# Two pairs of token blocks that take turns by halves of the inner tiles, in a spectral mixer with an MLP on one Trainium2 core

## The chip, the core and the metric

The kernel runs on 1 core of a Trainium2 chip. TensorE (PE in the profile; PEld is its weight load) multiplies, VectorE (DVE), ScalarE (ACT) and GpSimd (POOL) work elementwise, SyncE (SP) issues nearly all DMAs from one queue that it works off in order. The metric is the time of one execution on the device in microseconds (us).

## The reference

```python
X = np.fft.rfft(x, axis=1)                    # x: 8 x 3072 x 256
Yr = Xr @ w_r - Xi @ w_i + b_r                # complex 256 x 256 mix
Yi = Xr @ w_i + Xi @ w_r + b_i
Y  = sign(Y) * maximum(abs(Y) - 0.01, 0)      # real and imaginary part each
y  = np.fft.irfft(Y, n=3072, axis=1)          # tokens: 24576 x 256
h  = y @ w_in                                 # 256 -> 2048
g  = maximum(h, 0) + log1p(exp(-abs(h)))      # softplus
out = g @ w_out                               # 2048 -> 256
```

## The kernel before

All data is fp32. From the second batch on, and in the MLP throughout, a factor is split into a high part (fp32r, `hi`) and the rest (`lo`), and `mm3` (L207) issues three matmuls: hi by hi, hi by lo, lo by hi.

**The transform** of a batch goes in five steps of products, each with its evacuations: `s1` (16 products over the 96 points), `s3` (12, the 32 points), `mix` (12, the 256 x 256 mix with bias and shrinking), `s4` (12), `s5` (4 for each pair of token blocks). Between s1 and s3 the data goes through DRAM (`a_dr`), between s4 and s5 as well (`d_dr`, read back as `dp` tiles by `load_d`).

**The MLP** works on a *key* (batch, pair, mp): a pair of two token blocks of 512 tokens (3 pairs in a batch) and one of 8 inner tile pairs of 256 of the 2048 inner columns. The first layer of a key is 7 products in place of 8 (sums of weight blocks S1 to S4 and of token blocks T1 to T4): for one pair `s5` gives four PSUM tiles, and `b11`, `b12`, `b22`, `b21` (L496 to L518) make from them the seven split token tiles in `y_sb`. ACT and DVE snap, add and softplus the results (L530 to L554, tiles `psc` and `pse`), split them (`gh`, `gl`), and the second layer (`ffn2`, L556) adds them up in PSUM (`pso`, 2 banks for a block, 4 in all) over the 8 mp of a pair. After the last one `ffn2` copies the sums out into two `ot` tiles for a block and stores them.

**The weights** of the first layer (`w_in`, `which` = 1) and of the second (`which` = 0) come in 8 pieces each. A conversion, `split_w` (L146), turns one piece into float, sums and hi and lo parts in several steps on ACT, DVE and POOL, writes them in the tile `wp` (one buffer; `w_1` in the tile y1 for w_in while the start lasts), and stores them in DRAM (`w_dr`, L195). Its helper tile `wu` (L155) has the buffers of `ot` (tag "ot", two). `stream_w` (L200) reads a piece back for each key.

**The order** is written out by hand in *slots*. A key has four slots; slot 0 is the first of the MLP, and the slots before it are the start. In a slot the engines get, in this order: the first-layer products (`slot_products`), the due steps of conversions (`before`: a `yield` puts the rest into the next slot), at most one product of the transform (`steps`), loads and splits (`fill`), what an earlier slot put off (`later`), and the second-layer products (`slot_second`). Every engine works off its own list in order. The plan for the start is the list `first` (L671 to L681): s1 of batch 0 and four of batch 1, s3, mix and s4 of batch 0, six more s1 of batch 1, and s5 of pair 0. Nine conversions begin in the start, five slots apart, and seven more at slots 1, 4, ..., 19. Pair 1 of batch 0 is made ready (`plan_s5`) around slots 18 to 24, the remaining s1 of batch 1 run from slot 1, its s3, mix and s4 from slot 14.

Of the kernel before, what the change touches and what calls it, by code (L numbers as in the profile page):

```python
# [17 lines left out]
P = 128  # L18
# [3 lines left out]
BLK = 512  # L22
# [11 lines left out]
def tile_spectral_mixer_mlp(ctx, tc, x, w_r, w_i, bias, bias_0, w_in, w_out, f, f_hi, f_lo, g1, g3, g3_hi, g3_lo, hm, out):  # L34
# [61 lines left out]

    def store(dst, src, what):

        def start():
            nc.sync.dma_start(dst, src)  # L100
            stored[what] += 1

        later.append(start)
# [121 lines left out]
    def load_x(b, c):  # L225

        if b == 0 or (b, c // 10) == (1, 0):
# [15 lines left out]
    def s1(b, c):  # L243
# [17 lines left out]
        if b == 0:  # L261
            stored["a", b] += 1
        else:
            store(a_dr[b][:, 2 * c:2 * c + 2, :].rearrange("(g q) n c -> q g n c", q=4), a.rearrange("p (n c) -> p n c", n=2), ("a", b))

# [182 lines left out]
    def s5(b, blk, k):  # L448
# [3 lines left out]
        while t < (blk + 1) * BLK:  # L452
# [8 lines left out]
            t += n  # L461
        (b11, b21, b12, b22)[blk % 2 * 2 + k]((b, blk // 2), ps)

# [29 lines left out]
    def put_split(*args):  # L493
        split_token(*args) if early else later.append(lambda: split_token(*args))

# [7 lines left out]
    def b12(key, ps):  # L503
        difference(0, ps)
        keep(key, 1, ps)
        put_split(key, T1, 0, nc.vector if early else nc.gpsimd)

    def b22(key, ps):
        whole(key, B22, ps)
        difference(1, ps)  # L510
        difference(0, ps)
        put_split(key, T2, 0, nc.vector if early else nc.gpsimd)
        put_split(key, T3, 1, nc.vector)

    def b21(key, ps):
        whole(key, B21, ps)
        difference(0, ps)
        put_split(key, T4, 0, nc.vector if early else nc.gpsimd)  # L518

# [30 lines left out]
    def low(key, what):  # L550
# [64 lines left out]
    def slot_second(s, key, prev):  # L615
        if s < 3:
            if prev:
                what = (C22, C12, C21)[s]
                ffn2(prev, what, what == C22 and prev[2] == 0, what != C22 and prev[2] == NM // 2 - 1)
                if s == 2:  # L620
                    del w_t[0, prev]
        elif key:
            ffn2(key, C11, key[2] == 0, False)
            del w_t[1, key]


    with tc.manual_schedule():
# [17 lines left out]
        def plan_s1(b, start, step, first=0):  # L645
            for c in range(first, 16):
                t = product(start + step * (c - first), s1, b, c)
                at(t - 3, split_x, b, c)
                at(t - 7, load_x, b, c)

        def plan_mix(b, start, step):
            mixed = done = start
            for gp in range(NP):
                t = product(max(start + step * gp, mixed), s3, b, gp)
                at(max(t - 4, 11), load_a, b, gp)
                mixed = product(max(t + (3 if gp else 4), done + 1), mix, b, gp)
# [198 lines left out]
```

## Time and profile before

| | us |
|---|---|
| median of 3 runs | 2681.21 (2679.93 to 2683.26) |
| the profiled execution: its own time | 2679.82 |
| its span, first to last instruction | 2678.0 |
| PE busy | 2603.8 |

The trace of the profiled execution is read here by stages, cut at times at which a slot begins on PE: slot 0 at 131.07 us, slot 4 at 157.72, slot 16 at 205.46, slot 26 at 261.40 and slot 42 at 321.10. A view by stages gives each engine's busy time and the clock granted to TensorE (1.00 is 2.4 GHz). A view of waits names the instruction that waited and what released it. In a timeline the bracket behind a row is the idle time before it.

### The profile page before, as it was taken

What the parts mean: (1) busy time and instruction counts of PE and PEld (TensorE: products, weight loads), DVE (VectorE), ACT (ScalarE), POOL (GpSimd) and SP (SyncE); (2) the same over time, 40 slices, a digit from 0 to 9 for tenths busy, and PEclk for the clock granted to TensorE, in tenths of its full rate; (3) what the DMA queues carried; (4) which work ended last, traced back from release to release, by engine and by line L of the source; (5) the groups of instructions that cost most, each with busy time, mean ns of one, the idle gap of its engine ahead of it and who ended that gap; (6) DMA issues with size and microseconds to landing.
All of it is one profiled execution on the core that took longest, in us unless ns stands there. A gap on an engine that the chain in (4) does not pass through costs nothing.

```text
span 2678.0 us, 36264 instructions
## 1 busy us (share of the span) xinstructions
PE 2603.8 (97%) x13059; PEld 2184.2 (82%) x13059; DVE 1626.2 (61%) x2701; ACT 1719.5 (64%) x3115; POOL 301.3 (11%) x292
## 2 busy tenths in 40 slices
PE   7768999999999999999999999999999999999999
PEld 5546888888888888888888888888888888888887
DVE  3666665666646666566665666556665666645454
ACT  3365666666666666666676666666666666666665
POOL 2432110110101101101011011010010000000000
PEclk8889999999999999999999999999999999999999
DMA  6766556556455565564555644646455455445543
GB/s 191 254 210 206 194 164 198 166 187 193 157 188 178 178 198 170 179 205 156 184 172 172 217 159 153 220 163 198 164 167 191 155 170 188 142 154 183 186 147 110
DMA packets 186116, 479.73 MB, mean 179 GB/s; under 512 B 18097, under 2 KB 86961, under 8 KB 185937
## 3 DMA queue, kind: packets, MB, share of 16 engines
q1 hardware_dynamic: 185376, 476.95, 55.1%
q8 instruction: 103, 1.69, 0.3%
q0 software_dynamic: 560, 0.47, 0.1%
q14 instruction: 77, 0.62, 0.1%
HBM read 390.31 MB, written 83.89 MB: 177 GB/s over the span
## 4 chain that ended last, share of the span: by engine, by line
PE 88%; DVE 2%; DMA 2%; ACT 1%; issue 0%; POOL 0%; SPq 0%; DVEq 0%; ACTq 0%; POOLq 0%
PE pso L208 13%; PE pso L209 12%; PE pso L210 12%; PE psc L208 6%; PE psc L210 6%; PE psc L209 6%; PE pse L208 5%; PE pse L210 5%; PE pse L209 5%; PE psf L455 4%; PE psf L209 4%; PE psf L208 4%; PE psf L210 4%; PE psf L287 2%; DMA w_dr<-wp 1%; DVE shrunk L413 0%
## 5 line engine op out<-in xcount | busy, mean ns | idle before, releaser
L553 DVE TENSOR_TENSOR gl<-t,gh 128x512 fp32r<-128x512 f32 x768 | 533.2, 694 | 349.7 <-ACT gh L547 346.8
L532 ACT COPY t<-psc 128x512 f32<-128x512 f32 x576 | 337.0, 585 | 504.4 <-PE psc L210 502.4
L537 DVE TENSOR_TENSOR t<-pse,t 128x512 f32<-128x512 f32 x576 | 396.2, 688 | 426.9 <-ACT t L532 278.3
L208 PE MATMUL pso<-gh,w 128*128 128x512 f32 x1536 | 616.2, 401 | 0.0
L209 PE MATMUL pso<-gl,w 128*128 128x512 f32 x1536 | 600.0, 391 | 0.0
L210 PE MATMUL pso<-gh,w 128*128 128x512 f32 x1536 | 599.5, 390 | 0.0
L547 ACT CAST gh<-t 128x512 fp32r<-128x512 f32 x768 | 476.8, 621 | 58.2 <-PE pso L210 34.4
L543 ACT ACTIVATE t<-t 128x512 f32<-128x512 f32 x576 | 364.5, 633 | 58.7 <-DVE t L537 58.0
L210 PEld LDWEIGHTS pso<-gh,w 128*128 128x128 f32 x1536 | 288.7, 188 | 62.5
L208 PEld LDWEIGHTS pso<-gh,w 128*128 128x128 f32 x1536 | 290.1, 189 | 54.9
L209 PEld LDWEIGHTS pso<-gl,w 128*128 128x128 f32 x1536 | 290.0, 189 | 51.4
L208 PE MATMUL psc<-y_sb,w 128*128 128x512 f32 x768 | 301.6, 393 | 16.1 <-DMA w<-w_dr 7.8
L210 PE MATMUL psc<-y_sb,w 128*128 128x512 f32 x768 | 300.1, 391 | 0.0
L209 PE MATMUL psc<-y_sb,w 128*128 128x512 f32 x768 | 299.6, 390 | 0.0
L208 PE MATMUL pse<-y_sb,w 128*128 128x512 f32 x576 | 227.8, 396 | 14.4 <-DVE t L537 7.9
L115 POOL TENSOR_TENSOR xl<-xt,xh 96x512 fp32r<-96x512 f32 x102 | 134.1, 1317 | 938.3 <-ACT xh L106 783.6
L209 PE MATMUL pse<-y_sb,w 128*128 128x512 f32 x576 | 225.2, 391 | 0.0
L210 PE MATMUL pse<-y_sb,w 128*128 128x512 f32 x576 | 225.1, 391 | 0.0
L489 POOL TENSOR_TENSOR y_sb<-raw,y_sb 128x512 fp32r<-128x512 f32 x69 | 92.3, 1337 | 1128.5 <-ACT y_sb L486 1124.9
L208 PEld LDWEIGHTS psc<-y_sb,w 128*128 128x128 f32 x768 | 144.5, 188 | 51.0 <-ACT t L532 10.2
L210 PEld LDWEIGHTS psc<-y_sb,w 128*128 128x128 f32 x768 | 144.6, 188 | 31.0
L209 PEld LDWEIGHTS psc<-y_sb,w 128*128 128x128 f32 x768 | 144.6, 188 | 29.7
(131 smaller groups left out, 3637.8 us busy)
## 6 DMA issues: line engine op xcount, KB each, us to landing
w<-w_dr SPq DMA_DIRECT2D x192, 896.0 KB
w<-w_dr SPq DMA_DIRECT2D x192, 512.0 KB
dp<-d_dr SPq DMA_DIRECT2D x80, 384.0 KB
xt<-in_x SPq DMA_DIRECT2D x128, 192.0 KB
d_dr<-d SPq DMA_DIRECT2D x96, 256.0 KB
out_y<-ot SPq DMA_DIRECT2D x96, 256.0 KB
ap<-a_dr SPq DMA_DIRECT2D x84, 256.0 KB
a_dr<-a SPq DMA_DIRECT2D x102, 192.0 KB
```

The lines of the kernel that those rows point to most:

```text
L115: (eng or nc.vector).tensor_tensor(out=lo, in0=src, in1=hi.bitcast(F32), op=ALU.subtract)
L208: nc.tensor.matmul(ps, wh, xh, start=start, stop=False, skip_group_check=more)
L209: nc.tensor.matmul(ps, wh, xl, start=False, stop=False, skip_group_check=more)
L210: nc.tensor.matmul(ps, wl, xh, start=False, stop=stop, skip_group_check=more)
L287: nc.tensor.matmul(xv[:, g, k], t[:, g, k * P:(k + 1) * P], g1_t[:, g].rearrange("p (c s) -> p c s", c=2), start=True, stop=True,)
L455: nc.tensor.matmul(ps[:, t - blk * BLK:t - blk * BLK + n], d_sb[b, blk // 2, n2 // 4][0][:, n2 % 4, k * P:(k + 1) * P], d_sb[b, blk // 2, ...
L489: eng.tensor_tensor(out=lo, in0=raw[j], in1=hi.bitcast(F32), op=ALU.subtract)
L532: nc.scalar.copy(t, banks[bank])
L537: nc.vector.tensor_tensor(out=t, in0=banks[bank], in1=t, op=ALU.add)
L543: nc.scalar.activation(t, banks[bank] if bank else t, AF.Softplus)
L547: nc.scalar.copy(gh, ct[key, what])
L553: nc.vector.tensor_tensor(out=gl, in0=ct.pop((key, what)), in1=gh.bitcast(F32), op=ALU.subtract)
```

## The change

- **Turns.** In batch 0, pairs 0 and 1 take turns: pair 0 with mp 0 to 3, pair 1 with mp 0 to 3, pair 0 with mp 4 to 7, pair 1 with mp 4 to 7. Pieces 4 to 7 of the weights are first needed at slot 32 in place of slot 16.
- **Accumulators in DRAM.** After its first four mp a pair's sums are copied into `ot` tiles and stored (`part_dr`); `load_part` reads them back one slot ahead of the last products of the second half, and DVE adds them to PSUM in place of the copies.
- **Pair 1 earlier.** Its s5 products run in slots 2, 5, 7 and 10, its eight `dp` loads from slot -2.
- **Tokens of pair 0.** s5 runs in the order b11, b21, b12, b22, and `first_tokens` makes the tiles in another order of ACT and DVE instructions. B21 is kept in a third `raw` tile.
- **Conversions.** Six begin in the start, seven slots apart; ten more at slots 0, 3, 6, 10, 14, ..., 34. The store stands one step later.
- **The start** has four s1 of batch 1 behind s4 in place of six; these and the other s1 of batch 1 come from slot 0, loaded 5 slots ahead in place of 7.

```diff
 def load_w(which, m2):
-        if m2 < 6:
+        if m2 < 3:
 def split_w(which, m2):
         v.tensor_tensor(out=lo, in0=src, in1=hi.bitcast(F32), op=ALU.subtract)
+        yield
         nc.sync.dma_start((w1_dr if which else w2_dr)[m2][:, :], w.bitcast(F32))
 def s5(b, blk, k):
-        (b11, b21, b12, b22)[blk % 2 * 2 + k]((b, blk // 2), ps)
+        if early:
+            first_tokens((b, blk // 2), blk % 2 * 2 + k, ps)
+        else:
+            (b11, b21, b12, b22)[blk % 2 * 2 + k]((b, blk // 2), ps)
+    def first_tokens(key, i, ps):
+        v = nc.vector
+        if i == 0:
+            b11(key, ps)
+        elif i == 1:
+            whole(key, B21, ps)
+            raw[2] = sb.tile([P, BLK], F32, tag="d", name="raw")
+            nc.scalar.copy(raw[2], ps)
+        elif i == 2:
+            b12(key, ps)
+        else:
+            difference(0, ps)
+            difference(1, ps)
+            for j, t in ((0, T2), (1, T3)):
+                nc.scalar.copy(tokens(key, t)[0], raw[j])
+            nc.scalar.copy(tokens(key, B22)[0], ps)
+            for j, t in ((0, T2), (1, T3)):
+                hi, lo = tokens(key, t)
+                v.tensor_tensor(out=lo, in0=raw[j], in1=hi.bitcast(F32), op=ALU.subtract)
+            hi, lo = tokens(key, B22)
+            v.tensor_tensor(out=lo, in0=ps, in1=hi.bitcast(F32), op=ALU.subtract)
+            v.tensor_tensor(out=raw[2], in0=raw[2], in1=raw[0], op=ALU.subtract)
+            put_split(key, T4, 2, v)
+    def turns(key):
+        return key[:2] in ((0, 0), (0, 1))
+    def begins(key):
+        return key[2] == 0 or turns(key) and key[2] == NM // 4
+    def ends(key):
+        return key[2] == NM // 2 - 1 or turns(key) and key[2] == NM // 4 - 1
+    def load_part(blk):
+        partial[blk] = []
+        for k in range(2):
+            t = sb.tile([P, BLK], F32, name="part", **(dict(tag="d") if blk % 2 else dict(tag=f"r{k}", bufs=1)))
+            nc.sync.dma_start(t, part_dr[blk, k][:, :])
+            partial[blk].append(t)
 def ffn2(key, what, first, last):
                 ot = sb.tile([P, BLK], F32, tag="ot", name="ot")
-                if k == 0:
+                if blk in partial and not b:
+                    nc.vector.tensor_tensor(out=ot, in0=o[k], in1=partial[blk][k], op=ALU.add)
+                elif k == 0:
                     nc.scalar.copy(ot, o[k])
                 else:
                     nc.vector.tensor_copy(ot, o[k])
-                store(out[b, blk, k], ot, "out")
+                if mp == NM // 2 - 1:
+                    store(out[b, blk, k], ot, "out")
+                else:
+                    part_dr[blk, k] = dram.tile([P, BLK], F32, tag=f"part{blk}{k}", name="part_dr", bufs=1)
+                    store(part_dr[blk, k][:, :], ot, ("part", blk, k))
...
         for j in range(NM):
-            t = t0 + 23 + 5 * j if j < 9 else 1 + 3 * (j - 9)
+            t = t0 + 22 + 7 * j if j < 6 else 3 * (j - 6) if j < 8 else 6 + 4 * (j - 8)
...
         keys = [(b, bp, mp) for b in range(B) for bp in range(NPAIR) for mp in range(NM // 2)]
+        keys.sort(key=lambda key: (not turns(key), turns(key) and key[2] // (NM // 4), key))
+        for bp in range(2):
+            t = 4 * keys.index((0, bp, NM // 2 - 1))
+            at(t + 4, load_part, 2 * bp + 1)
+            at(t + 5, load_part, 2 * bp)
```

**ACT around the tokens of pair 0**, the last slots of the start; `y_80` is the s1 output of batch 1, `wu`, `w_962` and `wp` belong to a conversion. Before:

```order
L260 COPY y_80<-psf 96x512 x4
L474 CAST y_sb<-psf 128x512
L479 COPY raw<-psf 128x512
L158 ACTIVATE wu<-w_962 128x512
L161 ACTIVATE w_962<-w_962 128x512
L192 CAST wp<-wp 128x512
L479 COPY raw<-psf 128x512
L486 CAST y_sb<-raw 128x512
L474 CAST y_sb<-psf 128x512
L486 CAST y_sb<-raw 128x512 x2
L106 CAST xh<-xt 96x512
L474 CAST y_sb<-psf 128x512
```

The first L474 here is B11, the last one B21, which the second product of slot 0 needs. After:

```order
L261 COPY y_80<-psf 96x512 x3
L479 CAST y_sb<-psf 128x512
L484 COPY raw<-psf 128x512
L479 CAST y_sb<-psf 128x512
L509 COPY raw<-psf 128x512
L106 CAST xh<-xt 96x512
L192 CAST wp<-wp 128x512
L484 COPY raw<-psf 128x512
L491 CAST y_sb<-raw 128x512
L106 CAST xh<-xt 96x512
L516 CAST y_sb<-raw 128x512 x2
L517 CAST y_sb<-psf 128x512
```

B21 (the second L479) now comes second, and three copies of s1 stand ahead (of the stretch shown) in place of four.

**SP around slot 0**, up to the read of the first-layer weights for key 1 (`w1_dr1`). `xt` are the inputs of s1, `w64` raw weights, `w2_dr2` and `w2_dr3` stores of conversions. Before:

```order
L143 DMA w64_1043<-in_w_out 128x2x512
L231 DMA xt_1046<-in_x 96x512
L195 DMA w2_dr3_92<-wp_995 128x1024
L231 DMA xt_1071<-in_x 96x512
L143 DMA w64_1103<-in_w_in 128x2x512
L231 DMA xt_1106<-in_x 96x512
L204 DMA w1_1108<-w1_dr1_82 128x1792
```

After:

```order
L232 DMA xt_1006<-in_x 96x512
L442 DMA dp_1008<-in_hm 96x384
L443 DMA dp_1008<-d_dr_367 96x1024
L442 DMA dp_1011<-in_hm 96x384
L443 DMA dp_1011<-d_dr_367 96x1024
L442 DMA dp_1014<-in_hm 96x384
L443 DMA dp_1014<-d_dr_367 96x1024
L442 DMA dp_1017<-in_hm 96x384
L443 DMA dp_1017<-d_dr_367 96x1024
L232 DMA xt_1038<-in_x 96x512
L196 DMA w2_dr2_91<-wp_952 128x1024
L205 DMA w1_1069<-w1_dr1_82 128x1792
```

Eight loads for pair 1 (2.1 MB) and one store of a conversion have come ahead of the weights for key 1; two raw weight loads are gone from there.

**ACT where sums are copied out.** Before, this happens first in slots 33 and 34:

```order
L532 COPY t<-psc 128x512
L572 COPY ot<-pso 128x512
L532 COPY t<-psc 128x512
L330 COPY sum<-psf 128x256
L301 CAST lh<-psf 128x2x256
L106 CAST sh<-shrunk 128x512
L572 COPY ot<-pso 128x512
```

After, it happens first in slots 17 and 18:

```order
L303 CAST lh<-sum 128x2x128
L625 COPY ot<-pso 128x512
L562 COPY t<-psc 128x512
L158 ACTIVATE wu<-w_1637 128x512
L161 ACTIVATE w_1637<-w_1637 128x512
L625 COPY ot<-pso 128x512
L573 ACTIVATE t<-t 128x512
```

Between the two copies a conversion now takes one of the two `ot` buffers for `wu`, and holds it for two slots; the same happens in slots 33 and 34.

## Rows read from the trace of the kernel before

**Rows 1.** The page, engine totals: busy us, share of the span, instructions.

```profile
PE 2603.8 (97%) x13059; PEld 2184.2 (82%) x13059; DVE 1626.2 (61%) x2701; ACT 1719.5 (64%) x3115; POOL 301.3 (11%) x292
```

**Rows 2.** The view by stages, one row for each: from and to, length, busy time (and count) of PE, PEld, DVE, ACT and POOL, granted clock, DMA share, GB/s.

```profile
0.00:106.92 106.92, 85.95 (x451) 64.58 (x452) 60.12 (x96) 42.48 (x78) 38.13 (x42) 0.90 0.66 213
106.92:131.07 24.15, 17.52 (x61) 12.59 (x60) 6.32 (x13) 7.81 (x14) 7.40 (x9) 0.65 0.86 263
131.07:157.72 26.65, 11.71 (x34) 7.29 (x35) 17.77 (x29) 14.56 (x27) 11.07 (x10) 0.69 0.49 162
157.72:205.46 47.74, 38.76 (x156) 29.02 (x156) 31.79 (x58) 32.32 (x57) 14.49 (x10) 0.95 0.66 237
205.46:261.40 55.94, 44.54 (x222) 37.13 (x221) 36.39 (x64) 28.06 (x51) 12.00 (x15) 0.91 0.65 208
261.40:321.10 59.70, 59.04 (x310) 50.03 (x308) 42.70 (x76) 38.86 (x74) 5.15 (x4) 1.00 0.58 191
321.10:2678.00 2356.90, 2346.27 (x11833) 1983.52 (x11831) 1431.08 (x2369) 1555.37 (x2815) 213.09 (x204) 1.00 0.54 175
```

**Rows 3.** PE's timeline, single rows: start, length, instruction, idle time before it and its releaser.

```profile
119.88 1.99 PE L455 MATMUL psf<-dp 96*128 96x96 f32 x8 [5.95 <-DMA dp<-d_dr]
131.07 0.77 PE L208 MATMUL psc<-y_sb,w 128*128 128x512 f32 x1
...
139.20 0.79 PE L208 MATMUL pse<-y_sb,w 128*128 128x512 f32 x1 [6.50 <-ACT y_sb L474]
...
157.72 0.77 PE L208 MATMUL psc<-y_sb,w 128*128 128x512 f32 x1 [7.14 <-DMA w<-w_dr]
...
205.46 0.39 PE L208 MATMUL psc<-y_sb,w 128*128 128x512 f32 x1
205.69 0.39 PE L209 MATMUL psc<-y_sb,w 128*128 128x512 f32 x1
...
228.56 0.58 PE L208 MATMUL psf<-wmh,lh 128*128 128x256 f32 x1 [5.93 <-ACT raw L479]
```

**Rows 4.** ACT's timeline around the tokens of pair 0.

```profile
125.88 0.58 ACT L260 COPY y<-psf 96x512 f32<-96x512 f32 x1 [12.38 <-DMA a_dr<-y]
...
128.23 0.58 ACT L474 CAST y_sb<-psf 128x512 fp32r<-128x512 f32 x1
...
138.57 0.57 ACT L474 CAST y_sb<-psf 128x512 fp32r<-128x512 f32 x1
```

**Rows 5.** The timelines of POOL and of SP's queue ahead of slot 4, and last a line of SP's waits in the first 300 us (sum, times, longest).

```profile
149.39 1.31 POOL L165 TENSOR_TENSOR wu<-w,wu 128x512 f32<-128x512 f32 x1 [6.40 <-ACT xh L106]
150.65 3.39 POOL L115 TENSOR_TENSOR xl<-xt,xh 96x512 fp32r<-96x512 f32 x2
...
152.40 0.31 SPq L231 DMA_DIRECT2D xt<-in_x  x1
152.77 0.42 SPq L204 DMA_DIRECT2D w<-w_dr  x1
...
SPq L231 <- POOL xl L115: 17.8, 3, 8.5
```

**Rows 6.** The stage from 72 us to the last s4, by the view by stages.

```profile
72.00:106.92 34.92, 27.80 (x169) 22.02 (x168) 31.91 (x50) 13.42 (x25) 18.92 (x16) 0.95 0.77 255
```

**Rows 7.** A line of PE's waits in the first 262 us (sum, times, longest).

```profile
PE psf L427 <- POOL z L382: 4.9, 3, 2.2
```

**Rows 8.** DVE's groups from 131 to 262 us: count | busy, mean ns of one | idle before them and its releaser.

```profile
L194 DVE TENSOR_TENSOR wp<-wp 128x512 fp32r<-128x512 f32 (+1 forms) x8 | 6.7, 833 | 0.0
L163 DVE SCALAR_TENSOR_TENSOR wt<-wu,wt 128x512 f32<-128x512 f32 x8 | 5.5, 684 | 0.0
...
L160 DVE SCALAR_TENSOR_TENSOR wt<-w,wt 128x512 uint32<-128x512 uint32 x7 | 4.8, 693 | 0.2
L182 DVE TENSOR_TENSOR wp<-wt,wu 128x512 f32<-128x512 f32 x4 | 4.6, 1160 | 6.0 <-DMA w_dr<-wp 6.0
...
L164 DVE TENSOR_SCALAR wu<-wt 128x512 uint32<-128x512 uint32 x8 | 3.4, 427 | 0.3
...
L159 DVE TENSOR_SCALAR wt<-w 128x512 uint32<-128x512 uint32 x7 | 2.9, 420 | 0.0
...
L178 DVE TENSOR_TENSOR wp<-wt,wu 128x256 f32<-128x256 f32 x3 | 1.3, 426 | 10.1 <-DMA w_dr<-wp 10.1
```

**Rows 9.** Pieces of the chain that ended last, from 100 to 270 us: start, length, what.

```profile
216.49 8.79 DMA w_dr<-wp
240.79 4.63 DMA w_dr<-wp
253.91 1.31 PE psf L455 x12
262.24 0.89 PE psf L287 x8
```

**Rows 10.** The view of the tile `ot`, 280 to 310 us: durations min/median/max in ns, first and last start; last, who waited for its stores.

```profile
L572 ACT COPY ot<-pso x2: 587/594/601, 290.3 to 293.8; 128x512 f32<-128x512 f32 x2
L574 DVE COPY ot<-pso x2: 691/691/691, 292.5 to 295.4; 128x512 f32<-128x512 f32 x2
...
DVE ot L574: 0.6, 1
```

More of the change, by code (lines that the diff above doesn't have):

```diff
@@ L95, in put_off, with store @@
         later.append(f) if early else f()
-    def store(dst, src, what):
+    def store(dst, src, what, eng=None):
         def start():
-            nc.sync.dma_start(dst, src)
+            (eng or nc.sync).dma_start(dst, src)
             stored[what] += 1
@@ L225, in load_x @@
     def load_x(b, c):
-        if b == 0 or (b, c // 10) == (1, 0):
+        if b == 0 or (b, c // 8) == (1, 0):
             xt = sb.tile([P, 512], F32R, tag=("gh", "gl")[c % 2], name="xt", bufs=3).bitcast(F32)[:N1]
@@ L263, in s1 @@
         else:
-            store(a_dr[b][:, 2 * c:2 * c + 2, :].rearrange("(g q) n c -> q g n c", q=4), a.rearrange("p (n c) -> p n c", n=2), ("a", b))
+            store(a_dr[b][:, 2 * c:2 * c + 2, :].rearrange("(g q) n c -> q g n c", q=4), a.rearrange("p (n c) -> p n c", n=2), ("a", b),
+                  None)
     def load_a(b, gp):
@@ L493, in put_split @@
     def put_split(*args):
-        split_token(*args) if early else later.append(lambda: split_token(*args))
+        later.append(lambda: split_token(*args))
+    def first_tokens(key, i, ps):
[21 more added lines that the diff above has]
+            put_split(key, T4, 2, v)
     def b11(key, ps):
@@ L505, in b12 @@
         keep(key, 1, ps)
-        put_split(key, T1, 0, nc.vector if early else nc.gpsimd)
+        (split_token if early else put_split)(key, T1, 0, nc.vector if early else nc.gpsimd)
     def b22(key, ps):
@@ L511, in b22 @@
         difference(0, ps)
-        put_split(key, T2, 0, nc.vector if early else nc.gpsimd)
+        put_split(key, T2, 0, nc.gpsimd)
         put_split(key, T3, 1, nc.vector)
@@ L517, in b21 @@
         difference(0, ps)
-        put_split(key, T4, 0, nc.vector if early else nc.gpsimd)
+        put_split(key, T4, 0, nc.gpsimd)
     gt, po, ct, banks = {}, {}, {}, {}
@@ L554, in low @@
         gt[key, what] = gh, gl
+    def turns(key):
[4 more added lines that the diff above has]
+        return key[2] == NM // 2 - 1 or turns(key) and key[2] == NM // 4 - 1
+    part_dr, partial = {}, {}
+    def load_part(blk):
+        partial[blk] = []
+        for k in range(2):
+            assert stored["part", blk, k] == 1
+            t = sb.tile([P, BLK], F32, name="part", **(dict(tag="d") if blk % 2 else dict(tag=f"r{k}", bufs=1)))
+            nc.sync.dma_start(t, part_dr[blk, k][:, :])
+            partial[blk].append(t)
     def ffn2(key, what, first, last):
@@ L618, in slot_second @@
                 what = (C22, C12, C21)[s]
-                ffn2(prev, what, what == C22 and prev[2] == 0, what != C22 and prev[2] == NM // 2 - 1)
+                ffn2(prev, what, what == C22 and begins(prev), what != C22 and ends(prev))
                 if s == 2:
@@ L622, in slot_second @@
         elif key:
-            ffn2(key, C11, key[2] == 0, False)
+            ffn2(key, C11, begins(key), False)
             del w_t[1, key]
@@ L648, in plan_s1 @@
                 at(t - 3, split_x, b, c)
-                at(t - 7, load_x, b, c)
+                at(t - (5 if b == 1 else 7), load_x, b, c)
         def plan_mix(b, start, step):
@@ L654, in plan_mix @@
                 t = product(max(start + step * gp, mixed), s3, b, gp)
-                at(max(t - 4, 11), load_a, b, gp)
+                at(max(t - 4, 14), load_a, b, gp)
                 mixed = product(max(t + (3 if gp else 4), done + 1), mix, b, gp)
@@ L659, in plan_s5 @@
         def plan_s5(b, bp, start):
-            if (b, bp) == (1, 0):
+            if (b, bp) in ((0, 2), (1, 0)):
                 start += 3
@@ L667, in plan_s5 @@
                 t = product(t + 2, s5, b, 2 * bp + j, k)
-            assert t + 2 < NT * b + 2 * NM * bp, (b, bp, t)
+            assert t + 2 < NT * b + (NM if (b, bp) == (0, 1) else 2 * NM * bp), (b, bp, t)
         first = [("s1", 0, c) for c in range(16)] + [("s1", 1, c) for c in range(4)]
@@ L678, in tile_spectral_mixer_mlp @@
                 first.append(("mix", 0, i - 1))
-        first += [("s1", 1, c) for c in range(4, 10)]
-        first += [("s5", j, k) for j, k in ((0, 0), (1, 0), (1, 1), (0, 1))]
+        first += [("s1", 1, c) for c in range(4, 8)]
+        first += [("s5", j, k) for j, k in ((0, 0), (0, 1), (1, 0), (1, 1))]
         t0 = -len(first)
@@ L703, in tile_spectral_mixer_mlp @@
         for j in range(NM):
-            t = t0 + 23 + 5 * j if j < 9 else 1 + 3 * (j - 9)
-            at(t - (6 if j < 9 else 4 if j < 12 else 2), load_w, (j + 1) % 2, j // 2)
+            t = t0 + 22 + 7 * j if j < 6 else 3 * (j - 6) if j < 8 else 6 + 4 * (j - 8)
+            at(t - (6 if j < 6 else 8 if j < 7 else 2), load_w, (j + 1) % 2, j // 2)
             before.setdefault(t, []).append(split_w((j + 1) % 2, j // 2))
@@ L717, in tile_spectral_mixer_mlp @@
         nt = NT
-        plan_s1(1, 1, 1.6, 10)
+        plan_s1(1, 0, 1.6, 8)
         for b in range(B):
             for bp in range(1, NPAIR):
-                plan_s5(b, bp, nt * b + 2 * NM * bp - 14)
+                plan_s5(b, bp, nt * b + (NM if (b, bp) == (0, 1) else 2 * NM * bp) - 14)
             if b + 1 < B:
-                plan_mix(b + 1, *((14, 4.9) if b == 0 else (nt * b - 4, 5.6)))
+                plan_mix(b + 1, *((16, 4.9) if b == 0 else (nt * b - 4, 5.6)))
                 plan_s5(b + 1, 0, nt * (b + 1) - 14)
```

## The prediction

> **What bounds the kernel now.** I read the engine totals first. PE is busy 97% of the span [rows 1], so nothing that leaves its products alone can move the time except where PE waits or runs at the low clock. The view by stages says where that is [rows 2]: from 321.10 us on PE idles 10.6 us in 2357, and from slot 26 to 42 0.7 in 59.7, at a clock of 1.00. In the 261 us before, it idles 62.9 and the clock drops as far as 0.65. So the place of the change is the place of the loss, and only these stages need to be worked out.
>
> How much is lost there? One second-layer matmul follows another in 0.23 us at the full clock (the two rows at 205 us) [rows 3]. A key has 45 of them, 10.3 us, 2.6 a slot; key 0 has only 27 in its slots 0 to 3. An s1 is three, 0.7 us; an s5 takes 1.3 and an s3 0.9 [rows 9]. With these:
> - slots 0 to 3: 27 x 0.23 + 2 s1 = 7.6 us of work in 26.65: 19.0 lost;
> - slots 4 to 15: 12 x 2.6 + 4 s1 + an s3 = 34.9 in 47.74: 12.8 lost;
> - slots 16 to 25: slots 26 to 41, with the same transform work beside them, take 59.70 / 16 = 3.73 each; ten and four s5 are 42.5, in 55.94: 13.4 lost.
>
> The waits name the causes. Slot 0 has a product that waits 6.50 us for B21 [rows 3]: ACT copies it only at 138.57, after all other tiles; and ACT itself had stood 12.38 us behind stores of s1 output when s5 was already running, so that B11 came at 128.23, s5 having begun at 119.88 [rows 3, 4]. Slot 4 waits 7.14 us for its weights, which SP issued at 152.77, held up by an x load whose buffer waited for POOL, which had stood behind a conversion's multiply [rows 5]. In slots 4 to 25 DVE waits 6.0 + 10.1 = 16.1 us for the store of the conversion before, since `wp` has one buffer [rows 8]; the longest, a store of 8.79 us [rows 9], ends in PE's wait of 5.93 at 228.56 [rows 3]. Before all that, from 72 us to the last s4, DVE is busy 31.91 of 34.92 us, mostly with conversions, and PE 27.80 [rows 6].
>
> **The change part by part**, against the profiled execution (2679.82 us, 1.4 below the median).
>
> *1. Start: -6 us (0 to -11).* Six conversions for nine, every seventh slot for every fifth, take some 30% of DVE's conversion work out of a stage in which DVE is 91% busy and PE loses 7.1 us [rows 6], 4.9 of it over the start waiting for z, which comes through DVE [rows 7]. I take 4. Then s5 waits 5.95 us for `dp` [rows 3] with the DMA engines at a share of 0.86 [rows 2]; two raw weight loads (0.5 MB each), a weight store and two x loads leave: I take 2. If the wait is the latency of the last store and load, nothing comes; the upper end is 7.1 and two thirds of 5.95. The two s1 that leave had that wait behind them, so nothing is won by their going, and in slots they cost 2 x 0.7: *+1.4*.
>
> *2. Slots 0 to 3: -14.6 us (-6 to -19).* With four s1 in the start no copy waits for a store of the first four, so ACT is free when s5 ends its tiles; B21 is second, and the 6.50 goes. What is late next is the chain through T2: two differences, T2's copy and rest, T3's, B22's and T4's DVE work and the add of the first result, eight pieces of 0.6 to 0.7 (copies 0.58 in rows 4, DVE 0.68 in rows 8), 5.2; softplus, split and snap 1.8; product S1 and its snap 2; the add, the last two products at the low clock and the add for the next key 4, with a conversion's sums between, 1 more: 14 us. Work in it is 9.6 (one more s1, one s5), so 4.4 is lost for 19.0. The weights for key 1 stand behind eight `dp` loads now; 2.1 MB at the 263 GB/s of rows 2 are 8 us and the weights 3.5 more, about 12 after their first issue just ahead of slot 0: just in time. Low end: only the 6.50 goes. High end: all goes.
>
> *3. Slots 4 to 15: -1 us (-9 to +8).* Tokens of pair 1 (some eleven DVE and ten ACT pieces of 0.6 to 0.7) come in from slots 18 to 24; conversions are at three slots' distance until slot 6. There the next one writes `wp` one slot (3.7 us) after the last rest, and the store takes 4.6 to 8.8 [rows 9], as before: I expect one wait like the 8.37 hidden in the 10.1 of rows 8 around slot 5. From slot 10 on four slots' distance gives two slots (7.5 us) against 4.6: those waits go. Lost: 12 for 12.8.
>
> *4. Slots 16 to 41: +1 us (-10 to +35).* The 13.4 goes with the `wp` waits and with pair 1's tokens. Two things come. First, conversions now run to slot 39 beside s3, mix and s4. DVE is busy 42.70 / 16 = 2.67 us a slot there [rows 2]; a conversion has 3.7 us of DVE in the rows (29.2 us for some eight [rows 8]; the small sums of a w_in piece come on top), 0.9 a slot: 3.6 or more of 3.73. It fits, but an in-order engine that full makes PE wait: 8 us, an estimate from slots 4 to 15, where DVE at 31.79 of 47.74 went with 12.8 lost. Second, in slots 17, 18 and 33, 34 `wu` holds one of the two `ot` buffers, so the second block's two copies pass one after the other through the other buffer: copy, store, copy, store, copy. A store costs at most 2.2 us with little else queued, from the end of DVE's first copy (292.5 + 0.7) to the next, which waited for it at 295.4 [rows 10], 4.6 in company [rows 9]; copies are 0.6 and 0.7. The last copy is out 3.5 to 6.0 us after the last product; PE needs the bank after two first-layer products and one of the transform, some 2.8. So 0.7 to 3.2 a time; SP has a weight store and weights ahead, I take 3.2: 6.4. Sum 14.4 for 13.4.
>
> *5. The way back: +3 us (0 to +8).* The adds stand in for copies of the same length. But `load_part` is issued one slot ahead: for pair 0 its second half is behind weights (0.9 MB) and three `dp` pairs (1.6 MB), 10 us at 263 GB/s, with the add due in three slots, 11. DVE stands in order behind it with `gl` and the adds that PE needs: 2; for pair 1, with less ahead, 1. The trace of before has no such load; the nearest is the 4.6 of rows 9, with which it would be hidden. The Trainium skill, "DMA: Bandwidth & Descriptors", Rules for kernel authors, says the opposite of this placing: issue the DMA early, compute, wait late. Its fit of 2.0 us + bytes / 436 GB/s (section Anatomy of one DMA, taken on another queue) gives 4.1 us for a 0.9 MB store that took 4.63 here, and 9.6 for the second half: by it this term would be 0 to +1, and the sum 2 to 3 lower.
>
> The eight extra copies (0.6 each), 4 MB of DMA out and back and the longer second half of the weights lie in stages with DMA at 0.54 to 0.65 [rows 2] and ACT at two thirds: hidden; if not, 8 x 0.6.
>
> Sum: -6 + 1.4 - 14.6 - 1 + 1 + 3 = -16.2, so 2663.6 for a profiled execution, **2665** as a median.
>
> **Rivals.**
> *More: all `wp` waits go and DVE's load hides.* For it: slots 26 to 41 lose nothing with DVE at 72%. Terms 3 and 4 would be -10 and -10: 2665 - 20 = 2645.
> *The first wait is replaced.* If the x loads and conversion store that now stand before key 1's weights are late, as the x load was that waited up to 8.5 us [rows 5], or the `dp` loads fill the DMA engines longer, slot 4 begins 25 us after slot 0 and not 14. That gives 2676, within 0.2%. Against it: the first two x splits now stand ahead of the conversion's multiply on POOL.
> *DVE becomes the bound in slots 16 to 41, slower than before.* If the pace of slots 16 to 25, 5.6 us a slot, came not from `wp` but from conversions, mix and second-layer splits crossing on DVE, the change stretches it over 26 slots: 26 x (5.6 - 3.73) = 49 lost for the 14 of term 4, 2700. It decides from a pace of 3.73 + (14.4 + 16) / 26 = 4.9. For it: the sum of 3.6 or more of 3.73, and L182, 1160 ns where other 512-wide pieces take 690 [rows 8]. Against it: DVE was idle a third of slots 16 to 25. The Trainium skill, "GPSIMD Engine Reference", section 1 Specifications, has VectorE and GpSimd share SBUF interfaces, with contention where a DVE instruction has two SBUF inputs. The mean of L182 agrees; by that rule every DVE piece beside a POOL multiply stretches and this rival gains.
>
> **How the numbers follow.** Chances: forecast 0.64, more 0.12, replaced wait 0.14, DVE bound 0.10. The forecast's own range is 2652 to 2675. The range goes to 2645, where the second case lies, and over the third to 2684, half way to the last. What a measurement can tell from no change is about 0.2%, 5.4 us: faster 0.76, same 0.14, slower 0.10.
>
> **What would show it.** Step 1: slot 0 begins near 125 us. Step 2: no product waits for B21, slot 4 begins 13 to 16 us after slot 0. Step 3: DVE waits for `w_dr` once for long, near slot 5, and hardly from slot 12 on. Step 4: slots 16 to 41 at some 4.2 us; second-layer products in slots 19 and 35 wait 2 to 4 us for copies. Step 5: an add waits for `part_dr`. I am wrong if slot 4 still begins 25 us after slot 0, if slots 16 to 41 take 4.9 or more, or if a wait appears past slot 68.

## The result

The changed kernel takes **2708.8 us** (median of 4 runs, 2704.2 to 2709.5) against 2680.6 for the kernel before on the same chip (4 runs, 2679.5 to 2683.3): ratio 1.010, 95% interval 1.0083 to 1.0118. It is slower by 28 us; the prediction said 16 us faster, and its range ended at 2684.

The page's engine totals of the changed kernel, in the columns of [rows 1]:

```profile
span 2706.2 us, 36340 instructions
PE 2616.3 (97%) x13061; PEld 2192.6 (81%) x13061; DVE 1635.0 (60%) x2716; ACT 1725.3 (64%) x3118; POOL 298.0 (11%) x287
```

PE idles 2706.2 - 2616.3 = 89.9 us where it idled 74.2 [rows 1], 15.7 more. It is also busy 12.5 us longer with the same products (13061 records, 13059 before): their granted clock was lower, 0.979 over the span where it had been 0.987. Together they are the 28.2 us by which the span grew.

Where? The view by stages of the changed kernel, in the columns of [rows 2], cut where slots 0, 4, 16, 42 and 72 begin on PE:

```profile
104.50:124.39 19.89, 17.29 (x58) 12.36 (x57) 5.61 (x9) 8.21 (x14) 3.75 (x5) 0.59 0.80 240
124.39:145.30 20.91, 17.16 (x51) 12.20 (x50) 12.57 (x25) 12.75 (x25) 7.17 (x6) 0.61 0.96 284
145.30:206.94 61.64, 43.15 (x188) 33.51 (x187) 37.10 (x57) 36.29 (x66) 20.37 (x13) 0.86 0.51 169
206.94:331.04 124.10, 102.20 (x476) 82.71 (x475) 90.00 (x164) 72.99 (x133) 21.86 (x21) 0.89 0.61 210
331.04:460.00 128.96, 115.45 (x578) 96.71 (x576) 80.64 (x136) 73.52 (x134) 11.78 (x9) 0.93 0.54 173
460.00:2706.00 2246.00, 2237.65 (x11272) 1892.95 (x11270) 1355.94 (x2243) 1482.69 (x2677) 199.93 (x194) 1.00 0.54 175
```

In the kernel before the same slots begin at 131.07, 157.72, 205.46, 321.10 [rows 2] and, slot 72, at 433.48, by this row of PE's timeline:

```profile
433.48 0.39 PE L208 MATMUL psc<-y_sb,w 128*128 128x512 f32 x1
```

Stage against stage:

| stage | before | after | difference | the prediction's term |
|---|---|---|---|---|
| start, to slot 0 | 131.1 | 124.4 | -6.7 | -6 |
| slots 0 to 3 | 26.7 | 20.9 | -5.7 | -14.6 |
| slots 4 to 15 | 47.7 | 61.6 | +13.9 | -1 |
| slots 16 to 41 | 115.6 | 124.1 | +8.5 | +1 |
| slots 42 to 71 | 112.4 | 129.0 | +16.6 | +3 |
| from slot 72 | 2244.5 | 2246.2 | +1.7 | 0 |

(The prediction's +1.4 for two s1 moved into slots is in no one stage.) The gain at the beginning is there, though smaller; the loss lies at five places. PE's timeline of the changed kernel, as in [rows 3]:

```profile
171.30 0.79 PE L209 MATMUL psc<-y_sb,w 128*128 128x512 f32 x1 [13.00 <-ACT t L562]
...
225.81 0.74 PE L209 MATMUL psc<-y_sb,w 128*128 128x512 f32 x1 [2.71 <-ACT t L573]
226.34 0.63 PE L210 MATMUL psc<-y_sb,w 128*128 128x512 f32 x1
226.77 0.63 PE L211 MATMUL psc<-y_sb,w 128*128 128x512 f32 x1
231.75 0.80 PE L209 MATMUL pse<-y_sb,w 128*128 128x512 f32 x1 [4.36 <-DVE t L567]
...
238.75 0.39 PE L209 MATMUL psc<-y_sb,w 128*128 128x512 f32 x1
...
306.06 0.80 PE L209 MATMUL pse<-y_sb,w 128*128 128x512 f32 x1 [7.39 <-DVE t L567]
...
372.65 0.80 PE L209 MATMUL pse<-y_sb,w 128*128 128x512 f32 x1 [5.75 <-DVE t L567]
...
443.00 0.80 PE L209 MATMUL pse<-y_sb,w 128*128 128x512 f32 x1 [5.07 <-DVE t L567]
```

The wait of 13.00 ends where slot 7 begins. The others lie in slots 20, 36, 52 and 68, each time at the first `pse` product, two slots after the last products of a turn. These four slots take 12.9, 15.0, 11.0 and 12.7 us (slot 20: 225.81 to 238.75); in the fastest run below they take 6.1, 7.4, 3.4 and 4.9. The brackets name ACT and DVE, but both were waiting themselves. DVE's timeline says for what:

```profile
152.23 1.08 DVE L194 TENSOR_TENSOR wp<-wp 128x896 fp32r<-128x896 f32 x1
153.24 1.80 DVE L583 TENSOR_TENSOR gl<-t,gh 128x512 fp32r<-128x512 f32 x1
168.34 0.69 DVE L182 TENSOR_TENSOR wp<-wt,wu 128x512 f32<-128x512 f32 x1 [13.29 <-DMA w_dr<-wp]
...
229.81 0.69 DVE L627 COPY ot<-pso 128x512 f32<-128x512 f32 x1 [7.38 <-DMA part_dr<-ot]
...
304.11 0.69 DVE L627 COPY ot<-pso 128x512 f32<-128x512 f32 x1 [9.06 <-DMA part_dr<-ot]
...
370.08 1.31 DVE L623 TENSOR_TENSOR ot<-pso,part 128x512 f32<-128x512 f32 x2 [6.08 <-DMA out_y<-ot]
...
439.44 0.69 DVE L623 TENSOR_TENSOR ot<-pso,part 128x512 f32<-128x512 f32 x1 [5.93 <-DMA out_y<-ot]
```

One wait is for the store of a conversion, whose `wp` the next one wants; four are for stores of results, whose `ot` buffers are wanted again. In slots 52 and 68 the second block's results wait for the stores of the first block's. In slots 20 and 36 the last result waits for the store of the one just before it, of the same block: `wu` of a conversion held the other buffer. ACT made that copy, and had itself waited for a store before, to give `wu` its buffer (2.76 us, until 222.40; PE's 2.71 ahead of slot 20 stands behind that):

```profile
223.50 0.58 ACT L625 COPY ot<-pso 128x512 f32<-128x512 f32 x1
```

Behind these four waits stands, in DVE's order, the add of a first-layer result (L567) that frees the bank PE needs; behind the wait for `wp` stands a difference of tokens (L487, 168.95), which ACT's copy of `psc` (L562) came after. And SP's queue, where these stores were issued:

```profile
154.52 0.37 SPq L143 DMA_DIRECT2D w<-in_w_in  x1
156.19 0.32 SPq L232 DMA_DIRECT2D xt<-in_x  x1
156.60 0.38 SPq L205 DMA_DIRECT2D w<-w_dr  x1
157.03 0.61 SPq L100 DMA_DIRECT2D a_dr<-a  x1
157.74 0.41 SPq L196 DMA_DIRECT2D w_dr<-wp  x1
...
224.29 6.56 SPq L100 DMA_DIRECT2D part_dr<-ot  x2
...
361.44 1.24 SPq L604 DMA_DIRECT2D part<-part_dr  x2
363.02 1.86 SPq L100 DMA_DIRECT2D out_y<-ot  x2
```

Conversion 6's store could have gone at 153.3, when its rest was done; it stood 4.4 us behind a raw weight load, which waited for POOL, and an x load, and then took 10.6 (157.74 to 168.34) with 1.8 MB issued just ahead of it. It is the change that put it there: the `yield` ahead of the store moves it from slot 4 to slot 5, behind the loads of slot 4. No run takes that line back by itself. The stores of `ot` took 229.81 - 224.29 = 5.5 us and 370.08 - 363.02 = 7.1; before, at most 2.2 [rows 10].

### The profile page after: what moved, and what is told of

Read it like the earlier page. It is cut to its first block, busy times and chain, and to the rows that moved or that the text cites. A ratio compares the mean times of both kernels' runs of the same rounds, so it can differ in the third digit from the quotient of the medians.

```text
span 2706.2 us, 36340 instructions
## 1 busy us (share of the span) xinstructions
PE 2616.3 (97%) x13061; PEld 2192.6 (81%) x13061; DVE 1635.0 (60%) x2716; ACT 1725.3 (64%) x3118; POOL 298.0 (11%) x287
## 4 chain that ended last, share of the span: by engine, by line
PE 81%; DVE 1%; ACT 1%; DMA 1%; issue 0%; SPq 0%; DVEq 0%
PE pso L209 12%; PE pso L211 12%; PE pso L210 12%; PE psc L209 6%; PE psc L211 6%; PE psc L210 6%; PE pse L209 4%; PE pse L211 4%; PE pse L210 4%; PE psf L457 4%; PE psf L210 3%; PE psf L209 3%; PE psf L211 3%; PE psf L289 2%; DVE shrunk L415 0%; DMA out_y<-ot 0%
## 5 line engine op out<-in xcount | busy, mean ns | idle before, releaser
L583 DVE TENSOR_TENSOR gl<-t,gh 128x512 fp32r<-128x512 f32 x768 | 536.3, 698 | 333.6 <-ACT gh L577 330.7
L567 DVE TENSOR_TENSOR t<-pse,t 128x512 f32<-128x512 f32 x576 | 396.1, 688 | 437.0 <-ACT t L562 284.1
L562 ACT COPY t<-psc 128x512 f32<-128x512 f32 x576 | 337.8, 586 | 480.6 <-PE psc L211 478.7
L210 PEld LDWEIGHTS psc<-y_sb,w 128*128 128x128 f32 x768 | 145.4, 189 | 29.8
```

The source lines that it names most:

```text
L210: nc.tensor.matmul(ps, wh, xl, start=False, stop=False, skip_group_check=more)
L562: nc.scalar.copy(t, banks[bank])
L567: nc.vector.tensor_tensor(out=t, in0=banks[bank], in1=t, op=ALU.add)
L583: nc.vector.tensor_tensor(out=gl, in0=ct.pop((key, what)), in1=gh.bitcast(F32), op=ALU.subtract)
```

## The experiments

Each time is a median beside runs of the kernel before on the same chip (2680.5 to 2680.9), with the ratio to it. Stage lengths are read as above, from the starts of slots in each trace. In the runs that leave the changed start as it is (all but start_only and warm) slot 0 begins between 119.5 and 124.7 us; differences of a few us there are taken as scatter, so causes are read from single stages.

| run | us | ratio (95%) | slots 0-3 | 4-15 | 16-41 | 42-71 |
|---|---|---|---|---|---|---|
| before | 2680.6 | 1 | 26.7 | 47.7 | 115.6 | 112.4 |
| after | 2708.8 | 1.010 (1.0083 to 1.0118) | 20.9 | 61.6 | 124.1 | 129.0 |
| own_ot | 2685.5 | 1.0021 (1.0012 to 1.0029) | 20.4 | 62.7 | 109.3 | 124.2 |
| later7 | 2699.4 | 1.0071 (1.0059 to 1.0084) | 20.2 | 47.2 | 131.7 | 128.5 |
| both | 2674.6 | 0.9976 (0.9967 to 0.9986) | 20.5 | 45.3 | 113.0 | 124.7 |
| start_only | 2679.7 | 0.9997 (0.9988 to 1.0006) | 21.1 | 50.8 | 119.2 | 110.0 |
| part_early | 2700.7 | 1.0077 (1.0063 to 1.0091) | 20.0 | 61.9 | 123.5 | 125.1 |
| phase | 2687.8 | 1.0023 (1.0013 to 1.0032) | 21.3 | 50.9 | 115.4 | 128.3 |
| **in_place** | **2654.2** | **0.9902 (0.9888 to 0.9915)** | 20.7 | 47.0 | 103.2 | 110.3 |
| pair1_later | 2659.6 | 0.9922 (0.991 to 0.9935) | 15.4 | 58.1 | 106.1 | 110.2 |
| warm | 2655.3 | 0.9905 (0.989 to 0.9921) | 20.2 | 46.1 | 105.9 | 110.3 |

**own_ot: the second block's results in buffers of their own.**

```diff
-                ot = sb.tile([P, BLK], F32, tag="ot", name="ot")
+                if turns(key) and blk % 2 == 0:
+                    ot = partial[blk][k] if blk in partial else sb.tile([P, BLK], F32, tag=f"r{k}", name="ot", bufs=1)
+                else:
+                    ot = sb.tile([P, BLK], F32, tag="ot", name="ot")
```

> The changed kernel, but the second block's results at a turn's end no longer use the two `ot` buffers: in the first turns they go into the tiles `r0`, `r1`, in the last turns the sum is written in place over the part that was loaded. Theory A (results wait for a store to free one of two `ot` buffers, DVE stands in order behind that): in the changed kernel's trace slots 20, 36, 52 and 68 took 12.9, 15.0, 11.0 and 12.7 us, where a slot beside the same work takes about 4.2, so up to 35 us are to be had; I expect 28 of them, 2681 us, with no DVE wait of over 2 us on a store of `ot`. Theory B (DVE too full with conversions, and the part comes back late): the four slots keep over half of their excess, 2695 or more.

23 us of the 28 came; in the two traces 19.6 lie in slots 16 to 71, and some 5 ahead of slot 0, which the edit does not touch. DVE's waits for DMAs from 115 to 470 us (sum, times, longest) are now:

```profile
DVE wp L182 <- DMA w_dr<-wp: 13.0, 1, 13.0
DVE part L626 <- DMA part<-part_dr: 8.7, 3, 5.0
DVE ot L626 <- DMA part<-part_dr: 2.7, 1, 2.7
DVE wp L178 <- DMA w_dr<-wp: 2.2, 1, 2.2
```

None is for a store of `ot`; theory A holds for slots 20 and 36 (7.4 us each). But slots 52 and 68 still took 10.0 and 9.0: with the first wait gone, the adds waited for the part's load. Two waits had run side by side there, and only the longer one showed.

**later7: conversion 7 in slot 6, the following ones three slots later.**

```diff
-            t = t0 + 22 + 7 * j if j < 6 else 3 * (j - 6) if j < 8 else 6 + 4 * (j - 8)
+            t = t0 + 22 + 7 * j if j < 6 else 6 * (j - 6) if j < 8 else 9 + 4 * (j - 8)
```

> The changed kernel, but conversion 7 starts in slot 6 instead of 3 and those from the eighth on three slots later. Theory A (the wait of 13.3 us of DVE, and of 13.0 of PE behind it, is for conversion 6's store, which has one slot's time): the wait falls below 3 us and slot 7 starts some 11 us earlier, 2698 us. Theory B (the next conversion meets the same wait, or the added distance runs into the deadline of the last ones): 2706 to 2712, with a wait of over 8 us for `w_dr` somewhere between slots 4 and 42.

The wait is gone (DVE waits for `w_dr` once more, 1.7 us), and slots 4 to 15 fell by 14.4. Slots 16 to 41 became 7.6 longer: in the new phase a conversion begins in slot 17 and takes an `ot` buffer before the *first* block's results, and DVE's waits for `part_dr` stores rose from 16.4 to 28.3. So the whole gained 9 and not 14.

**both edits.**

> Both edits. Theory A: the two causes are separate, so the gains add: 2708.8 - 28 - 11 = 2670, faster than the kernel before. Theory B: 2695 or more. If the sum falls short by over 8 us, one wait stood behind the other.

It gained 34.2 of the 39 expected; the two gains alone add up to 23.3 + 9.4 = 32.7, so the causes are separate.

**start_only: the kernel before with the new start and tokens, nine conversions ahead, no turns.**

```diff
-        if b == 0 or (b, c // 10) == (1, 0):
+        if b == 0 or (b, c // 8) == (1, 0):
...
-        (b11, b21, b12, b22)[blk % 2 * 2 + k]((b, blk // 2), ps)
+        if early:
+            first_tokens((b, blk // 2), blk % 2 * 2 + k, ps)
+        else: ...
...
-        first += [("s1", 1, c) for c in range(4, 10)]
-        first += [("s5", j, k) for j, k in ((0, 0), (1, 0), (1, 1), (0, 1))]
+        first += [("s1", 1, c) for c in range(4, 8)]
+        first += [("s5", j, k) for j, k in ((0, 0), (0, 1), (1, 0), (1, 1))]
...
-            t = t0 + 23 + 5 * j if j < 9 else 1 + 3 * (j - 9)
+            t = t0 + 22 + 5 * j if j < 9 else 1 + 3 * (j - 9)
```

> The kernel before with the change's start alone: eight s1 of the second row in it and not ten, the first tokens in the new order, nine conversions ahead as before, no turns. Theory A (the tokens' order and the s1 that leave make slots 0 to 3 shorter by some 6 us, the six conversions instead of nine bring the earlier slot 0): slots 0 to 3 in 21 us, slot 0 at 130, 2675 us. Theory C (both come from the three conversions that leave): 2679 to 2683, slots 0 to 3 in 25 us or more.

Slots 0 to 3 took 21.1 us with all nine conversions ahead, 5.5 less than before, so the tokens' order and the s1 shorten them by themselves, as theory A has it (this run has neither the `dp` loads nor the s5 of pair 1 there); slot 0 began at 128.1, 3 us earlier, so half or more of the start's gain needs the conversions to leave. The whole is no faster. That is the time that theory C forecast, but not by its cause: slots 4 to 41 took 6.6 us more. PE's timeline of this run has a new wait in slot 16, for the s1 output of batch 1:

```profile
215.92 2.05 PE L288 MATMUL psf<-ap 128*128 128x128 f32 x8 [12.75 <-DMA ap<-a_dr]
```

SP issued this load at 208.46, behind the eight `dp` loads for pair 1 (from 201.47); in the kernel before it went at 195.18, ahead of them. The run keeps the changed kernel's plan of s3 for batch 1, with loads from slot 14 in place of 11, which the cut above does not show.

**part_early: the even blocks' parts loaded at slots 44 and 62.**

```diff
-            at(t + 5, load_part, 2 * bp)
+            at((44, 62)[bp], load_part, 2 * bp)
```

> The changed kernel, but the even blocks' parts are loaded at slots 44 and 62 instead of 49 and 65, nothing else. The prediction's step (the add waits for its part): slots 52 and 68 lose 8 us or more of their 11.0 and 12.7 together, 2700 us or less. Theory A (the add waits first for `ot`, whose store is late; the part's load is hidden behind that): under 5 us together, 2704 to 2709, DVE still waiting some 12 us for the stores of `ot`.

The median fell by 8.0, between the two expectations; but slots 42 to 71 fell only by 3.9, and most of the rest lies ahead of them (slot 42 began 3.2 earlier), in stages that the edit does not touch. At the place itself it is theory A's "under 5". DVE still waited there for the stores, 8.9 us where it had been 12.9:

```profile
DVE ot L623 <- DMA out_y<-ot: 8.9, 2, 4.6
```

**phase: conversions away from slots 18 and 34, `ot` as it was.**

```diff
-            t = ... 3 * (j - 6) if j < 8 else 6 + 4 * (j - 8)
+            t = ... 4 * (j - 6) if j < 8 else 7 + 4 * (j - 8)
```

> The changed kernel, but conversions 8 to 15 start in slots 7, 11, ... 35 instead of 6, 10, ... 34, so that none holds an `ot` buffer in slots 18 and 34; conversion 7 starts in slot 4 instead of 3. Prediction's mechanism (the conversion's `wu` in one of the two buffers makes three results pass through the other): slots 20 and 36 fall from 12.9 and 15.0 to some 7 each, -13, and the wait at slot 7 falls by one slot, -3: 2692. Rival (two buffers are too few for four results with stores of 5.5 to 7 us, with or without `wu`): slots 20 and 36 keep 11 or more each, 2701 to 2706.

Neither number fits whole. Slots 20 and 36 take 8.0 and 10.9 us (12.9 and 15.0), but slot 19 grew from 5.6 to 8.5. DVE's waits for `part_dr` stores halve (16.4 to 7.8): `wu` is about half of the chain, two buffers for four results the rest. Slot 7 surprised: one slot more for conversion 7 and PE's 13.0 us wait was gone, slots 4 to 15 down by 10.8. In this run the store is issued at the end of its rest and ahead of the raw weight load, and DVE waits 3.2:

```profile
148.18 0.34 SPq L196 DMA_DIRECT2D w_dr<-wp  x1
151.40 0.38 SPq L143 DMA_DIRECT2D w<-in_w_in  x1
```

One slot of distance was expected to take 3 us off the wait, and 10 went. The store's new place on SP fits the rest; the run changed both, so their shares are not shown.

**in_place: no result waits for a store or a fresh load.** With later7's plan of conversions:

```diff
+                if blk in partial and not b:
+                    ot = partial[blk][k]
+                else:
+                    where = (dict(tag="ot"), dict(tag="r0", bufs=1), dict(tag="r1", bufs=1), dict(tag="d"))
+                    ot = sb.tile([P, BLK], F32, name="ot", **where[(1 - blk % 2) * 2 + k if turns(key) else 0])
...
-            t = sb.tile([P, BLK], F32, name="part", **(dict(tag="d") if blk % 2 ...
+            t = sb.tile([P, BLK], F32, name="part", **(dict(tag="ot") if blk % 2 ...
...
-            at(t + 4, load_part, 2 * bp + 1)
-            at(t + 5, load_part, 2 * bp)
+            at((44, 60)[bp], load_part, 2 * bp + 1)
+            at((45, 62)[bp], load_part, 2 * bp)
```

> Conversions 7 to 15 three slots later as in the run before, and no result at a turn's end waits for a store or a load that was just issued: first turns use `ot`, `r0`, `r1` and one `d` tile, last turns add in place over parts that were loaded at slots 44 and 45 (pair 0) and 60 and 62 (pair 1) instead of 48, 49, 64 and 65. In the run with both edits slots 19, 52 and 68 still took 9.8, 10.5 and 8.8 us, with 8.1 us of DVE waiting for the store of a part and 11.6 for its load. Theory A (those are the last of the same two causes): they fall to about 4.5 each, 2674.6 - 14 = 2660 us. Rival (the loads, now in slots 44 and 60, delay weights or transform data there, or DVE is late at a turn's end without any wait for a DMA): 2668 or more.

20 us below the run with both edits where 14 were expected, and 1% below the kernel before: the fastest of all. DVE waits for no DMA from 115 to 470 us. Its view by stages, slots 16 to 41 and 42 to 71:

```profile
190.34:293.58 103.24, 95.56 (x475) 78.30 (x474) 94.73 (x168) 74.37 (x135) 18.85 (x21) 0.98 0.74 250
293.58:403.86 110.28, 109.36 (x577) 92.79 (x576) 80.57 (x136) 73.35 (x134) 12.05 (x9) 1.00 0.64 206
```

Beside the changed kernel's 124.10 and 128.96 the two stages shortened by 20.9 and 18.7 us, while PE's busy time in them fell by 6.6 and 6.1: a third of the loss was the clock (0.89 and 0.93 there, 0.98 and 1.00 here). Slots 20, 36, 52 and 68 take 6.1, 7.4, 3.4 and 4.9.

**pair1_later: in_place with pair 1's tokens and their `dp` loads three slots later.**

```diff
-            if (b, bp) in ((0, 2), (1, 0)):
+            if (b, bp) in ((0, 1), (0, 2), (1, 0)):
```

> The run with results in place, but the tokens of pair 1 and the eight `dp` loads for them three slots later. In the changed kernel's trace slots 0 to 3 took 20.9 us, and ACT stood 3.7 and 2.1 us in them for x loads that SP issued behind the `dp` loads, with the DMA engines at 0.96. Theory A (that queue holds the slots back): slots 0 to 3 fall from 20.7 to 17 or less, the whole by 3 us or more, 2651 us. Rival (the low clock and the chain of the first tokens hold them, the loads were hidden): slots 0 to 3 at 20 or more, 2653 to 2658, slower if the loads now collide with weights in slots 1 to 7.

Slots 0 to 3 fell to 15.4, as theory A forecast, but not by its mechanism: PE idled 4.6 us in them, where it idles 3.3 in in_place. What fell is its busy time, 17.4 to 10.9: one s5 (2.71 us there) left these slots, and the granted clock was 1.00 from 128 us on, where in_place has 0.61 over the stage. Whether the loads or that s5 had kept the clock down is not shown. And the time was not saved (the traced execution is 4.6 us above the median). ACT's timeline, one slot later:

```profile
151.53 0.58 ACT L261 COPY a<-psf 96x512 f32<-96x512 f32 x1 [9.54 <-DMA a_dr<-a]
```

The same eight loads, issued at 138.6 to 142.3 now, held up the stores of s1 output behind them, ACT stood for those, and slot 4 took 13.0. The loads and tokens cost at both places tried; 5 us more here.

**warm: in_place with 24 useless products ahead of the first s5** (extra work, written into a bank that s5 overwrites).

```diff
+        if early and not blk and not k:
+            for _ in range(24):
+                nc.tensor.matmul(ps[:, :D], wmh[:, 0, 0, :P], wmh[:, 1, 0, :], start=True, stop=True)
```

> The run with results in place, but 24 products of 256 columns without use are put on PE ahead of the first s5, into the bank that it then overwrites: about 2.8 us at the full clock, 5.2 at half, partly in its wait for `dp`. In the changed kernel s5 and most of slots 0 to 3 ran at half clock after PE had idled 9 us in 99 to 114. Theory D (busy PE there brings the full clock back by slot 0): 48 s5 products in 5 to 6 us instead of 10.6, first-layer products of slot 0 at 0.23 us instead of 0.43, and the time falls by 4 us or more. Rival (waits go on, and so does the half clock): slot 0 begins 2 to 5 us later, 2655 to 2659.

No difference (2655.3 to 2654.2). PE's timeline shows why:

```profile
105.27 3.44 PE L455 MATMUL psf<-wmh 128*128 128x256 f32 x24
111.41 1.10 PE L460 MATMUL psf<-dp 96*128 96x96 f32 x8 [2.71 <-DMA a_dr<-y]
113.75 8.79 PE L460 MATMUL psf<-dp 96*128 96x96 f32 x40 [1.23 <-DMA dp<-d_dr]
```

The products ran at the full clock (0.14 us each) and so did the first eight of s5 (1.10 / 8 = 0.14); after the next wait, 1.23 us, the other 40 took 0.22 each, at a granted clock of 0.50, and slot 0 began at that clock. Work put into one wait did not help past the next.

## Why the prediction was wrong

The stage of the change, the waits of the kernel before and the direction of the first two terms were read rightly. The steps that failed are terms 2 to 5: each came out 7 to 15 us worse than forecast, and with them the sign.

1. **Start, -6:** measured -6.7 (-6.3 to -11.6 over the runs with the same start). Right, if small.
2. **Slots 0 to 3, -14.6:** measured -5.7. B21's wait went, as said. The weights were "just in time". The step that failed is the price of the products: the sum has the low clock for the last two, six of the 27 matmuls, and most of the 27 ran at it. PE was busy 17.2 us with what the prediction counts as 9.6 us of work, at a granted clock of 0.61, and idled only 3.7. An x load was late behind the `dp` loads, too, at a DMA share of 0.96: issued at 129.76, it kept ACT waiting for 3.69 us (its row stands below the list). ACT's other wait for an x load, the 2.1 us in the expectation of pair1_later, ended at 123.50, before the first `dp` load was issued. pair1_later shows that 15 can be had, without that s5 and at the cost of the next slots.
3. **Slots 4 to 15, -1:** measured +13.9. The place was foreseen ("one wait like the 8.37 hidden in the 10.1 of rows 8 around slot 5"), the size was not: 13.3 us of DVE, 13.0 of PE. The prediction took the store's length and left out the store's place on SP, one step later than before and so behind a load that waits for POOL's step of the very conversion that wants `wp`. later7 and phase move that and take 14.4 and 10.8 back.
4. **Slots 16 to 41, +1:** measured +8.5. "I take 3.2: 6.4", between a store of 2.2 us and one of 4.6 "in company", was the mis-sized part; in place of 6.4 the chain cost 124.1 - 103.2 = 20.9 (later7's plan of conversions is also in that difference). The buffers were passed on as it says, copy, store, copy, store, copy; but no second-layer product waited for that in slots 19 and 35. The adds stood behind the last copy in DVE's order, and the first `pse` products of slots 20 and 36 waited, 4.36 and 7.39 us. The stores took 5.5 to 6.4 us, for DMA engines that carried weights as well (a share of 0.83 from 224.29 to 229.81), and each wait brought half clock behind it. The other part, 8 us for DVE's load, is not contradicted: in_place loses 103.2 - 26 x 3.73 = 6.2 in all, with DVE 92% busy.
5. **The way back, +3:** measured +16.6; in_place gives back 18.7. The step priced the part's load alone. It overlooked that in the last turns, too, the second block's adds need the `ot` buffers of the first, and those stores were queued behind the part's loads. Before, the copies met the same two buffers with stores of 2.2 us [rows 10] and waited 0.6; that row was read as the price of a store and not as its price on an idle queue.

ACT's row for term 2, the x load behind the `dp` loads:

```profile
138.63 0.62 ACT L106 CAST xh<-xt 96x512 fp32r<-96x512 f32 x1 [3.69 <-DMA xt<-in_x]
```

The Trainium skill, "DMA: Bandwidth & Descriptors", section Anatomy of one DMA, has 2.0 us + bytes / 436 GB/s, taken on another queue, 2.6 us for these 256 KB. The kernel before is a little below it (at most 2.2); the changed kernel is far above it (5.5 to 7.1; from 358 to 374 us the engines were 88% busy). The same page's Rules for kernel authors, issue early and wait late, which the prediction set against the placing of `load_part`, is what part_early does for half of the loads (-3.9 us in their stage).

Three small slips of the prediction bear on nothing above: by that fit of the Trainium skill (the same section) the load of pair 0's second half (0.9, 1.6 and 0.5 MB) is estimated at about 9 us and not 9.6; half way from 2665 to 2700 is 2682.5 and not 2684; and the two rows at 205 us are first-layer products, which are as long as second-layer ones.

Of the rivals, "the first wait is replaced" was the nearest in kind, though not in place. "DVE becomes the bound" gave nearly the right time for the wrong reason: slots 16 to 41 took 4.8 us each, but DVE was busy 90.0 of 124.1 us, and in_place runs the same DVE work (94.7) in 103.2. DVE did not bind; it stood. Whether pair 1's loads can stand anywhere without a cost stays open: two places were tried.

## What to carry to other kernels

Before a change adds a second visit to a rotating buffer, write down for each visit who holds every buffer then, when its store is issued (what stands ahead on that queue, and what that waits for) and how busy the DMA engines are: a store's price from a quiet stage was wrong by a factor of about 3 here. Results that are added to something already loaded can be written over it, which needs no buffer at all. When a change that should win loses, look for the waits on its path first: here the idea was worth 1%, and hid behind waits for `wp`, for `ot` and for the parts read back.

## What the runs showed of the hardware

- Waits cost more here than their length. The waits of 4.36, 7.39, 5.75 and 5.07 us in slots 20, 36, 52 and 68 are 22.6 us; beside in_place these slots lost 6.8, 7.6, 7.6 and 7.8, 29.8 us (slot 36 has another wait of 0.96, and one of 2.13 in in_place). The granted clock in them was 0.60, 0.61, 0.69 and 0.70, in in_place 1.00, 0.77, 1.00 and 1.00. From 225.81 on products follow each other in 0.43 us in place of 0.23, the half clock. In the run warm the clock fell after a wait of 1.23 us that came 1.1 us after one of 2.71.
- DVE beside POOL: L583 took 1.80 us at 153.24 while POOL multiplied (152.45 to 154.49); its mean over the run is 0.70. The Trainium skill, "GPSIMD Engine Reference", section 1 Specifications, names the shared SBUF interfaces; the trace agrees. It names them for DVE instructions with two SBUF inputs, not for every piece, as the prediction has it: L567, with one input in PSUM, took 0.69 at 233.51 while POOL multiplied (232.90 to 234.52).
